# An RWKV and soft-MoE kernel on one core: gathers ahead of the bulk loads, y added by VectorE alone, logits behind the state product, the first slot reordered, the tail in four column groups

## The chip, the core and the metric

The kernel runs on one core of one Trainium2 chip. Its five engines work in parallel, each through its own instruction list in program order: TensorE (PE in the profile; PEld is its weight load), VectorE (DVE), ScalarE (ACT), GpSimd (POOL) and SyncE (SP), which here only issues DMA transfers. An engine waits for another through semaphores. SBUF is the working memory of 128 partitions; PSUM, with 8 banks, takes what TensorE writes. The metric is the time of one execution in microseconds on the device.

## The reference

The inputs are r, k, v, w of shape (4, 8, 768, 48) (batch, head, time, head dimension), u (8, 48), phi (384, 32), w1 (8, 384, 1024) and w2 (8, 1024, 384), all float32.

```
state = 0                                            # per batch and head, 48 x 48
for t in range(768):
    y[t]  = r[t] @ (state + outer(u * k[t], v[t]))
    state = w[t][:, None] * state + outer(k[t], v[t])
x = y as (3072 rows = batch x time, 384 columns = head x dimension)

logits = x @ phi                                     # 3072 x 32 slots, 4 slots for each of 8 experts
d = softmax of logits over the 3072 rows;  slot_input = d.T @ x           # 32 x 384
slot_out[e] = relu(slot_input[e] @ w1[e]) @ w2[e]    # per expert, 4 slots each
c = softmax of logits over the 32 slots;   out = c @ slot_out             # 3072 x 384
```

Both softmaxes add 1e-9 to the sum. The output is stored transposed, 384 x 3072.

## The kernel before, in words

**Attention in 16 slots.** Slot j (0 to 15) works on batch b = j // 4 and on two heads, g = j % 4. Time is cut into 6 chunks of 128 steps. Within a chunk the recurrence is a matrix product: with the running products of w inside a chunk, k is scaled by one (G, from a backward scan, g_scan) and r by another (a forward scan, f_scan), so that the scores of a chunk are k_scaled.T @ r_scaled, masked, and times v; the part across chunks goes through the state at the chunks' ends. w, k and r come in twelve units, three for each batch: a unit has 112 partitions of two heads (48 each, at partitions 0 and 64) and, in the 2 x 16 left-over partitions, a third of two further heads. So slots with g < 3 read a unit's tile directly (kr_b), and slots with g = 3 (3, 7, 11 and 15) read the tile g4, which **gather(n)** (line 516) puts together from the left-over rows of the three units of the batch with two DMAs of 16 rows each, SBUF to SBUF, 96.4 KB a DMA, 24 in all. A gather of unit n has to wait until k and r of unit n are scaled.

**A slot on each engine.** TensorE: the transposes of scaled k (e_kn, line 579, 5 of them), the scores in two halves (e_scores, 589), the sum of k and v per chunk (e_u, 625), the product of the previous slot's masked scores with v (e_av, 648, into the two banks y0 and y1), in some slots the transposes of finished x (x_turn, line 96), the logits (101), the slot product (s_mm, 140), the u-term (e_a, 605), then the previous slot's state product (e_inter, 659, into the same y banks), and one dummy matmul (fill, 497). VectorE: masked copies of three of the four score tiles (598), the state scan (633), reciprocal and forward scan (f_scan, 537 and 538), backward scan (g_scan, 530). ScalarE: evictions from PSUM. The fourth score tile goes by ScalarE (594) and a select on GpSimd (595). GpSimd: r * k (p_rk, 545), k scaled (p_k, 549), r scaled (p_r, 553), v times the u-term (p_av, 620, into the tile av). y of a slot (c_y, 666) is y0 and y1 plus av: ScalarE copies y0 to SBUF (668) and GpSimd adds av to it (670); VectorE adds av to y1 (669).

**Transfers.** All loads but one are issued by SyncE, in program order, into one hardware queue. Per unit: w (387.5 KB, ld_w), k and r (768 KB, ld_kr; the first three units go to other tiles by ld_raw); per slot v (288 KB, ld_v); per expert w1 in three pieces of 512 KB (ld_w1, line 687) and w2 likewise (ld_w2, 690). The tuple PIECES says how many w1 pieces are issued in a slot, in the function weights. A DMA into a tile waits on SyncE's list until the last readers of that tile are done, and all later DMAs of the list wait behind it: w of a unit for c_chk (560, ScalarE, after f_scan) and p_r, v for e_av and p_av, k and r for the state product and the gathers that read the old contents. Unit 0's k and r are issued by ScalarE instead, in two halves, beside SyncE's first loads.

**The MoE part.** The softmax over rows is kept running over the batches (s_max, s_exp, s_sum, s_acc); a batch's logits are computed in the slots of the next batch. After slot 15 comes a chain for the last batch: y (c_y_last), transposes, logits, maximum, exponent, the product d.T @ x, the merge into SI (s_acc), the slot input for the experts (m_slots), the up product (line 224: 8 experts x 3 row blocks x 2 halves of 512 columns), relu and transposes of h (turn, 239), the down product (257) in three groups of 128 columns (COLS), each scaled by the softmax sum (so_scale, 264), spread over partitions (so_rep, 267), and multiplied by the transposed c (mix, 282), copied to SBUF by VectorE and ScalarE (288, 286) and stored. w1 and w2 use SBUF tiles (bin 0 to 15) that the attention part has given free; W1_BINS and W2_BINS say which.

## Time and profile before

| | us |
|---|---|
| median of 3 runs (lowest, highest) | 212.97 (210.42, 213.46) |
| the profiled execution | 212.05 |
| its span in the profile | 210.2 |
| TensorE busy (share of the span) | 177.1 (84%) |
| VectorE busy | 115.7 (55%) |
| GpSimd busy | 104.5 (50%) |
| ScalarE busy | 72.2 (34%) |
| moved by DMA | 51.79 MB, 246 GB/s over the span |

The profile's first page gives busy time by engine, the span in 40 slices with TensorE's granted clock (full speed is 2.4 GHz, the other level 1.2 GHz) and the DMA engines' busy share, the chain of work that ended last, and groups of instructions by source line. Further views are cut from the same execution: tables of busy time in chosen stretches, timelines of one engine with the idle time before a row and what ended it (in brackets), and the times of DMAs from issue to landing. Matmuls overlap, so the time from one row's start to the next row's start says more than a row's own length.

### The profile page before, as it was taken

What the parts mean: (1) busy time and instruction counts of PE and PEld (TensorE: products, weight loads), DVE (VectorE), ACT (ScalarE), POOL (GpSimd) and SP (SyncE); (2) the same over time, 40 slices, a digit from 0 to 9 for tenths busy, and PEclk for the clock granted to TensorE, in tenths of its full rate; (3) what the DMA queues carried; (4) which work ended last, traced back from release to release, by engine and by line L of the source; (5) the groups of instructions that cost most, each with busy time, mean ns of one, the idle gap of its engine ahead of it and who ended that gap; (6) DMA issues with size and microseconds to landing.
All of it is one profiled execution on the core that took longest, in us unless ns stands there. A gap on an engine that the chain in (4) does not pass through costs nothing.

```text
span 210.2 us, 7632 instructions
## 1 busy us (share of the span) xinstructions
PE 177.1 (84%) x3306; PEld 133.2 (63%) x3308; DVE 115.7 (55%) x207; ACT 72.2 (34%) x202; POOL 104.5 (50%) x108
## 2 busy tenths in 40 slices
...
GB/s 177 381 231 298 205 222 303 30 271 168 296 278 305 215 28 362 149 297 263 311 333 85 210 128 323 306 313 385 154 342 416 409 407 260 74 50 254 211 312 93
DMA packets 15176, 51.79 MB, mean 246 GB/s; under 512 B 2208, under 2 KB 2976, under 8 KB 14752
## 3 DMA queue, kind: packets, MB, share of 16 engines
...
q10 hardware_dynamic: 544, 0.79, 1.3%
...
## 4 chain that ended last, share of the span: by engine, by line
PE 54%; DMA 24%; DVE 8%; POOL 5%; issue 2%; SPq 1%; ACT 1%; ACTq 0%; DVEq 0%; POOLq 0%
DMA bin<-bin 14%; PE sc L589 10%; PE y L648 8%; DMA bin<-in_w1l_dram 6%; PE so L257 5%; PE hp L224 5%; DMA bin<-in_krl_dram 4%; PE xp L96 4%; PE up L625 3%; PE kp L579 3%; PE y L659 3%; PE sp L140 3%; PE op L282 2%; POOL bin L553 2%; PE ap L605 2%
## 5 line engine op out<-in xcount | busy, mean ns | idle before, releaser
L589 PE MATMUL sc<-bin 48*128 48x128 f32 x384 | 34.3, 315 | 5.0 <-ACT bin L581 2.8
L589 PEld LDWEIGHTS sc<-bin 48*128 48x128 f32 x384 | 29.4, 215 | 9.7 <-ACT bin L581 4.9
L598 DVE COPY_PREDICATED bin<-later,sc 128x384 f32<-128x384 int32 x49 | 25.3, 581 | 13.4 <-PE sc L589 13.4
L648 PE MATMUL y<-bin,bin 128*64 128x48 f32 x768 | 29.3, 238 | 0.6 <-issue 0.2
L549 POOL TENSOR_TENSOR bin<-bin,bin 128x768 f32<-128x768 f32 (+1 forms) x13 | 20.3, 1563 | 18.7 <-issue 11.6
L648 PEld LDWEIGHTS y<-bin,bin 128*64 128x64 f32 x768 | 27.7, 155 | 1.2 <-ACT bin L668 0.5
L530 DVE TENSOR_TENSOR_SCAN bin<-bin,cst 128x775 f32<-128x775 f32 (+2 forms) x13 | 21.2, 1628 | 2.4 <-DMA bin<-in_wl_dram 2.4
L545 POOL TENSOR_TENSOR bin<-bin 128x768 f32<-128x768 f32 x12 | 21.8, 1819 | 0.1
L538 DVE TENSOR_TENSOR_SCAN bin<-bin,cst 128x774 f32<-128x774 f32 (+1 forms) x13 | 21.4, 1643 | 0.5
L497 PE MATMUL zero<-zb 128*128 128x512 bf16 x58 | 19.8, 443 | 1.5 <-DVE cst L713 1.3
L579 PE MATMUL kp<-ident,bin 112*128 112x112 f32 x80 | 12.0, 287 | 9.3 <-DMA bin<-bin 4.7
L579 PEld LDWEIGHTS kp<-ident,bin 112*128 112x128 f32 x80 | 9.8, 155 | 11.8 <-issue 9.5
L670 POOL TENSOR_TENSOR bin<-bin,bin 128x288 f32<-128x288 f32 x15 | 10.6, 705 | 12.7 <-ACT bin L668 8.0
L620 POOL TENSOR_TENSOR bin<-bin,asb 128x576 f32<-128x576 f32 x12 | 14.0, 1165 | 3.8 <-ACT asb L608 1.7
L581 ACT COPY bin<-kp 128x336 f32<-128x336 f32 (+1 forms) x32 | 11.1, 397 | 13.4 <-PE kp L579 13.4
L595 POOL TENSOR_SCALAR_AFFINE_SELECT bin<-bin 128x384 f32<-128x384 f32 x15 | 7.8, 520 | 15.8 <-ACT bin L594 15.8
L594 ACT COPY bin<-sc 128x384 f32<-128x384 f32 x15 | 7.2, 478 | 22.4 <-PE sc L589 21.3
L633 DVE TENSOR_TENSOR_SCAN bin<-up,bin 112x288 f32<-112x288 f32 x16 | 12.0, 748 | 4.5 <-PE up L625 3.9
L553 POOL TENSOR_TENSOR bin<-bin,bin 128x768 f32<-128x768 f32 (+1 forms) x9 | 13.7, 1518 | 0.0
L257 PE MATMUL so<-bin,bin 128*32 128x128 f32 x384 | 12.2, 274 | 0.0
L497 PEld LDWEIGHTS <-zb 128*128 128x128 bf16 x60 | 6.0, 110 | 9.2 <-issue 5.0
L257 PEld LDWEIGHTS so<-bin,bin 128*32 128x32 f32 x384 | 10.2, 110 | 2.0 <-issue 1.7
...
## 6 DMA issues: line engine op xcount, KB each, us to landing
...
bin<-in_wl_dram SPq DMA_DIRECT2D x11, 387.5 KB, 3.3
...
bin<-bin SPq DMA_DIRECT2D x24, 96.4 KB, 7.5
...
```

The source lines that it names most:

```text
L257: nc.tensor.matmul(out=so[32 * g:32 * g + NS, :], lhsT=hT[ft // 2].rearrange("p (f e s) -> p f e s", f=2, e=E)[:, ft % 2, e, :], rhs=w2t[e ...
L497: nc.tensor.matmul(out=z, lhsT=zb[:, 0:P], rhs=zb, start=True, stop=True)
L530: nc.vector.tensor_tensor_scan(out=G[:, a:z][:, ::-1], data0=wt[:, a:z][:, ::-1], data1=cst[:, 0:1].broadcast_to([P, z - a]), initial=1.0, ...
L538: nc.vector.tensor_tensor_scan(out=wt[:, a:z], data0=wt[:, a:z], data1=cst[:, 1:2].broadcast_to([P, z - a]), initial=1.0, op0=ALU.mult, op ...
L545: nc.gpsimd.tensor_tensor(out=rk_b[n % 2], in0=raw(n)[:, 0:S], in1=raw(n)[:, S:2 * S], op=ALU.mult)
L549: nc.gpsimd.tensor_tensor(out=io[0], in0=io[1], in1=chunks(G_b[n % 2], 2, lo, hi), op=ALU.mult)
L553: nc.gpsimd.tensor_tensor(out=io[0], in0=io[1], in1=chunks(w_b[n % 2], 0, lo, hi), op=ALU.mult)
L579: nc.tensor.transpose(out=kp[:, c - lo, :], in_=kr[0:PITCH, P * c:P * c + P], identity=ident[0:PITCH, 0:PITCH])
L589: nc.tensor.matmul(out=sc[h][:, c, :], lhsT=kr[head(h), lo:lo + P], rhs=kr[head(h), S + lo:S + lo + P], start=True, stop=True)
L598: nc.vector.copy_predicated(out=at, mask=later.broadcast_to([P, HC, P]), data=sc[h])
L620: nc.gpsimd.tensor_tensor(out=av, in0=vt(j), in1=a, op=ALU.mult)
L648: nc.tensor.matmul(out=yb[h][rows, c, :], lhsT=at[:, rows], rhs=vt(j)[:, h, c, :], start=(c == 0), stop=False)
```

## The change

Seven edits, none of which changes what is computed up to rounding order.

1. *Transfers.* In the slot loop, k and r (now of the unit used by slot j - 2) and the weight pieces are issued at the head of a slot, right after e_kn, and w and v later in the slot as before. In slots with g = 1 the weight pieces come at the slot's end instead, and the gather of the third unit, which was in the next slot, comes just ahead of them. PIECES is spread anew (21 pieces as before).
2. *y by VectorE.* c_y is two VectorE additions from PSUM; ScalarE's copy and GpSimd's addition are gone.
3. *Logits behind the state product.* In slots with g = 1 the logits, the maximum, the exponent and e_a come after e_inter and c_y, in the order logits, e_a.
4. *Within a slot.* f_scan comes after the first two masked copies instead of before them, p_r right behind it; c_ends moves from a slot's end to behind the scores of the next slot; the copy of the state (c_state) is split off from state and comes later on ScalarE. c_state, c_pat and c_chk keep their work.
5. *First slot.* Unit 0's k and r come from a second copy in HBM (kr0, the same numbers with each half of the chunks contiguous) on SyncE's queue, between the two halves of w; 14 filling matmuls instead of 26, and the first slot's transposes, sums and scores are taken apart with filling matmuls between.
6. *Softmax over slots.* The sum takes the 1e-9 from an extra column of the tile ce, in place of one VectorE instruction (173) per batch.
7. *Tail.* The last exponent in two halves; the slot input as two products accumulated in PSUM (old SI times the rescaled factor, and the new product, copied to SBUF, times the factor) in place of the merge and one product; the softmax sum after the first quarter of the up product; the first half's turn inside the last quarter of the up product, the other one inside the down product; the down product ordered by row block over all 8 experts, in halves; four column groups (128, 128, 64, 64), of which the narrow two use mix_narrow, with two output DMAs each, one of them issued by ScalarE.

```diff
-N_FILL0 = 26
-N_START = (4, 4, 4)
+N_FILL0 = 14
+N_START = (4, 4, 6)
-N_CHAIN = 2
-PIECES = (0, 0, 1, 1, 2, 1, 1, 2, 2, 2, 2, 2, 2, 2, 1, 0)
+PIECES = (0, 0, 1, 2, 2, 1, 2, 1, 2, 1, 2, 1, 2, 2, 2, 0)
-COLS = ((0, 128), (128, 256), (256, 384))
+COLS = ((0, 128), (128, 256), (256, 320), (320, 384))
...
@@ -248,17 +271,17 @@
-    def down_proj(hT, so, w2t, cg, a=0, z=2 * FT):
+    def down_proj(hT, so, w2t, cg, half):
         lo, hi = COLS[cg]
-        for n in range(a, z):
-            st_, ft = divmod(n, FT)
-            for g in range(4):
-                e = 4 * st_ + g
-                nc.tensor.matmul(
-                    out=so[32 * g:32 * g + NS, :], lhsT=hT[ft // 2].rearrange(
-                        "p (f e s) -> p f e s", f=2, e=E)[:, ft % 2, e, :],
-                    rhs=w2t[e][:, FT * lo + ft * (hi - lo):FT * lo + (ft + 1) * (hi - lo)],
-                    start=(n == 0), stop=(n == 2 * FT - 1))
+        for ft in range(4 * half, 4 * half + 4):
+            for st_ in range(2):
+                for g in range(4):
+                    e = 4 * st_ + g
+                    nc.tensor.matmul(
+                        out=so[32 * g:32 * g + NS, :], lhsT=hT[ft // 2].rearrange(
+                            "p (f e s) -> p f e s", f=2, e=E)[:, ft % 2, e, :],
+                        rhs=w2t[e][:, FT * lo + ft * (hi - lo):FT * lo + (ft + 1) * (hi - lo)],
+                        start=(ft == 0 and st_ == 0), stop=(ft == FT - 1 and st_ == 1))
...
+    def mix_narrow(cT, rep, o, row, bank):
+        ov = o.rearrange("p (n q t) -> p q n t", q=4, t=P)
+        ops = [bank(q, [P, 3, P], "op") for q in range(4)]
+        for hf in range(2):
+            for q in range(4):
+                nc.tensor.matmul(out=ops[q][HALF * hf:HALF * hf + HALF].rearrange("p n t -> p (n t)"),
+                                 lhsT=rep[32 * q:32 * q + NS, :],
+                                 rhs=cT[32 * q:32 * q + NS, 3 * P * hf:3 * P * hf + 3 * P], start=True, stop=True)
+        for q in range(4):
+            if q % 2:
+                nc.scalar.copy(out=ov[:, q], in_=ops[q])
+            else:
+                nc.vector.tensor_copy(out=ov[:, q], in_=ops[q])
+        nc.sync.dma_start(out=out[row:row + HALF, 0:1536], in_=o[0:HALF])
+        nc.scalar.dma_start(out=out[row:row + HALF, 1536:3072], in_=o[HALF:P])
...
-        nc.scalar.copy(out=dst, in_=ys[j][0])
-        nc.vector.tensor_tensor(out=y_of(j, 1), in0=ys[j][1], in1=av[:, 1], op=ALU.add)
-        nc.gpsimd.tensor_tensor(out=dst, in0=dst, in1=av[:, 0], op=ALU.add)
+        for h in range(2):
+            nc.vector.tensor_tensor(out=y_of(j, h), in0=ys[j][h], in1=av[:, h], op=ALU.add)
...
     ld_w(0, 0, HC)
-    ld_raw(0, 0, HC, nc.scalar)
+    ld_half(0)
     ld_w(0, HC, C)
-    ld_raw(0, HC, C, nc.scalar)
+    ld_half(1)
     ld_w(1)
     ld_raw(1)
...
+    spare = lambda shape, name: own(shape, name, "y1")
+    fill(N_FILL0, spare)
     for hf in range(2):
         g_scan(0, HC * hf, HC * hf + HC)
         f_scan(0, HC * hf, HC * hf + HC)
     g_scan(1)
-    f_scan(1)
     for hf in range(2):
         p_k(0, HC * hf, HC * hf + HC)
         p_r(0, HC * hf, HC * hf + HC)
     c_ends(0)
+    p_k(1)
+    e_scores(0, 0)
+    fill(N_START[0], spare)
+    e_kn(0)
     c_chk(0)
-    p_k(1)
+    f_scan(1)
     p_r(1)
-    c_ends(1)
+    fill(N_START[1], spare)
+    c_pat(0)
+    e_u(0)
+    fill(N_START[2], spare)
+    e_scores(0, 1)
     c_chk(1)
-    for hf in range(2):
-        e_scores(0, hf)
-        fill(N_START[hf])
     ld_w(2)
     ld_w(3)
     ld_kr(3)
...
+        m = unit(j - 2) if j > 1 else None
+        m = m + 4 if m is not None and m + 4 < NU else None
+        nw = {0: n0 + 3, 1: n0 + 4, 3: n0 + 5}.get(g)
+        nw = nw if nw is not None and 4 <= nw < NU else None
         if j > 2:
             p_av(j - 1)
+        if j:
+            e_kn(j)
         if g == 1:
             gather(n0)
             gather(n0 + 1)
-        if g == 2:
-            gather(n0 + 2)
-        if ahead is not None:
+        if m is not None:
+            ld_kr(m)
+        if g != 1:
+            weights(PIECES[j])
+        if j == 1:
             f_scan(ahead)
-        e_kn(j)
         if j:
             e_scores(j, 0)
+            if ahead is not None and j > 1:
+                f_scan(ahead)
+            if ahead is not None:
+                p_r(ahead)
             e_scores(j, 1, ((1, 1), (0, 1))[0:SHARED[j]])
-        c_pat(j)
-        e_u(j)
+        if ends is not None:
+            c_ends(ends)
+        ends = later_g
+        if j:
+            c_pat(j)
+            e_u(j)
         state(j)
         if j:
             e_av(j - 1)
         if ahead is not None:
-            p_r(ahead)
             c_chk(ahead)
-        nw = {0: n0 + 3, 1: n0 + 4, 3: n0 + 5}.get(g)
-        if nw is not None and 4 <= nw < NU:
+        if nw is not None:
             ld_w(nw)
-        if j + 3 < NIT and j > 2:
-            ld_v(j + 3)
-        weights(PIECES[j])
         if g == 0 and pb >= 0:
             x_turn(pb, 1)
         if g == 1 and pb >= 0:
@@ -795,17 +866,16 @@
         if g == 2 and pb >= 0:
             s_dturn(qs[pb], rot)
             s_rows(qs[pb], rot)
-            s_rows_exp(qs[pb])
+            s_rows_exp()
+        c_state(j)
         if 1 <= j <= 2:
             e_a(j - 1)
             p_av(j - 1)
-        if j > 1 and unit(j) is not None:
+        if j + 3 < NIT:
+            ld_v(j + 3)
+        soft = g == 1 and pb >= 0
+        if j > 1 and unit(j) is not None and not soft:
             e_a(unit(j))
-        if g == 1 and pb >= 0:
-            lp = rot([TG, 2, P], "lp")
-            for kt in range(KT):
-                l_mm(kt, xT[:, kt], lp)
-            qs[pb] = s_max(pb, lp)
         if g == 3 and pb >= 0:
             sp = s_mm(x_b[pb % 2], qs[pb], rot)
             s_acc(pb, qs[pb], sp)
@@ -816,26 +886,27 @@
                 p_rk(later_g)
             p_k(later_g)
         if g == 2 and pb >= 0:
-            s_norm(pb, qs[pb])
+            s_norm(pb)
         if j:
             e_inter(j - 1)
             c_y(j - 1)
-        if g == 1 and pb >= 0:
+        if soft:
+            lp = rot([TG, 2, P], "lp")
+            for kt in range(KT):
+                l_mm(kt, xT[:, kt], lp)
+            qs[pb] = s_max(pb, lp)
             s_exp(pb, qs[pb])
             s_keep(qs[pb])
-        if later_g is not None:
-            c_ends(later_g)
+            e_a(unit(j))
         if j == 1:
             p_rk(1)
             p_rk(2)
         if j == 3:
             row_constants()
-        if j < 3:
-            ld_v(j + 3)
         fill(N_FILL[j])
-        m = unit(j - 1) if j else None
-        if m is not None and m + 4 < NU:
-            ld_kr(m + 4)
+        if g == 1:
+            gather(n0 + 2)
+            weights(PIECES[j])
         if j == 13:
             for i in range(KT):
                 ld_w1(E - 1, i)
...
@@ -869,35 +940,41 @@
-    fill(N_CHAIN)
     l_turn(x_b[lb % 2], 2, rot, evict2)
+    fill(2)
     l_mm(2, xT[:, 2], lp)
     q = s_max(lb, lp)
-    s_exp(lb, q)
-    fill(N_CHAIN)
+    s_exp(lb, q, 2)
+    fill(2)
     bc = m_spread(lb, rot)
+    s_dturn_parts(q, rot)
     m_factor(lb, q, bc)
-    s_dturn(q, rot)
-    fill(N_CHAIN)
     s_keep(q)
-    s_sum(lb, q)
+    fill(2)
     sp = s_mm(x_b[lb % 2], q, rot)
+    sT = rot([P, KT, NS], "sT")
+    m_old(q, sT)
...
-    s_acc(lb, q, sp)
-    fill(N_CHAIN)
-    m_slots(q, siT, rot)
-    fill(N_CHAIN)
-    m_den(q, rot)
+    spS = cut(2, X, DM)[0:TG]
+    nc.vector.tensor_copy(out=spS[:, 0:192], in_=sp[:, 0:192])
+    nc.scalar.copy(out=spS[:, 192:DM], in_=sp[:, 192:DM])
+    fill(2)
+    m_new(q, sT, spS)
+    ld_w2(6, 2)
+    m_slots(q, siT, sT)
+    fill(2)
     hps = [own([P, 512], f"hp{n}", f"y{n}") for n in range(2)]
     up_proj(siT, hps[0], w1t, 0, 0)
+    s_sum(lb, q)
+    m_den(q, rot)
...
@@ -931,41 +1007,50 @@
-    o_t = [w1t[2], w1t[3], w1t[4]]
-    sos = [own([P, P], f"so{cg}", ("up", "cst", "up")[cg]) if cg < 2 else None for cg in range(3)]
+    o_t = [w1t[2], w1t[3], w1t[4][:, 0:1536], w1t[4][:, 1536:3072]]
     any_bank = lambda q, shape, name: rot(shape, name)
...
+    sos = {}
+
+    def down(cg, half):
+        if half == 0:
+            sos[cg] = own([P, COLS[cg][1] - COLS[cg][0]], f"so{cg}", ("up", "cst")[cg % 2])
+        down_proj(hT, sos[cg], w2t, cg, half)
+        if half:
+            so_scale(sos[cg], so_sb[:, slice(*COLS[cg])])
 
     def spread(cg):
...
-    down_proj(hT, sos[0], w2t, 0)
-    scale(0)
-    for cg in range(1, 3):
-        if cg == 2:
-            sos[2] = own([P, P], "so2", "up")
-        down_proj(hT, sos[cg], w2t, cg, 0, 5)
-        spread(cg - 1)
-        down_proj(hT, sos[cg], w2t, cg, 5, 10)
-        mix_part(cg - 1, 0, any_bank)
-        if cg == 1:
-            range_check()
-        down_proj(hT, sos[cg], w2t, cg, 10, 15)
-        mix_part(cg - 1, 1, any_bank)
-        down_proj(hT, sos[cg], w2t, cg, 15, 16)
-        scale(cg)
...
+    down(0, 0)
+    c_turn(cT, 3, rot)
+    turn(h_sb, hT, 1, rot)
+    down(1, 0)
+    range_check()
+    down(0, 1)
+    down(1, 1)
+    spread(0)
+    down(2, 0)
+    wide(0, 0)
+    spread(1)
+    down(2, 1)
+    wide(0, 1)
     spread(2)
-    mix_part(2, 0, any_bank)
-    mix_part(2, 1, last_bank)
+    down(3, 0)
+    wide(1, 0)
+    narrow(2)
+    down(3, 1)
+    wide(1, 1)
+    spread(3)
+    narrow(3)
```

Three places of the instruction lists, as the two kernels have them.

SyncE's list around slot 9 (g = 1). bin_100 before and bin_103 after are g4; a row `16x1542 x2` is one gather; the rows in_w1l, in_krl, in_wl and in_vl are weight pieces, k and r, w and v. Before:

```order
L519 DMA bin_100<-bin_98 16x1542 x2
L519 DMA bin_100<-bin_99 16x1542 x2
L503 DMA bin_96<-in_wl_dram 128x775
L514 DMA bin_96<-in_vl_dram 128x576
L687 DMA bin_105<-in_w1l_dram 128x1024 x2
L506 DMA bin_98<-in_krl_dram 128x1536
L519 DMA bin_100<-bin_96 16x1542 x2
```

Now:

```order
L565 DMA bin_103<-bin_101 16x1542 x2
L565 DMA bin_103<-bin_102 16x1542 x2
L547 DMA bin_99<-in_wl_dram 128x775
L560 DMA bin_99<-in_vl_dram 128x576
L565 DMA bin_103<-bin_99 16x1542 x2
L742 DMA bin_108<-in_w1l_dram 128x1024
L550 DMA bin_101<-in_krl_dram 128x1536
```

The batch's last gather has moved from behind the weight pieces and k and r to in front of them.

VectorE's list from the end of slot 7 to the end of slot 8. `x3` and `x2` are masked copies of scores; the scans over bin and cst are g_scan (128x775) and f_scan (128x774), the one of 112x288 is the state; `128x6x48` is an addition of y. Before:

```order
L530 SCALAR_TENSOR_TENSOR bin_100<-bin_97,cst 128x775
L669 TENSOR_TENSOR bin_94<-y_1083,bin_99 128x6x48
L537 RECIPROCAL bin_97<-bin_100 128x6
L538 SCALAR_TENSOR_TENSOR bin_97<-bin_97,cst 128x774
L598 COPY_PREDICATED bin_101<-later,sc 128x384 x3
L633 SCALAR_TENSOR_TENSOR bin_95<-up,bin_95 112x288
```

Now:

```order
L576 SCALAR_TENSOR_TENSOR bin_103<-bin_100,cst 128x775
L725 TENSOR_TENSOR bin_97<-y_1074,bin_102 128x6x48
L725 TENSOR_TENSOR bin_97<-y_1075,bin_102 128x6x48
L653 COPY_PREDICATED bin_104<-later,sc 128x384 x2
L583 RECIPROCAL bin_100<-bin_103 128x6
L584 SCALAR_TENSOR_TENSOR bin_100<-bin_100,cst 128x774
L653 COPY_PREDICATED bin_104<-later,sc 128x384
L688 SCALAR_TENSOR_TENSOR bin_98<-up,bin_98 112x288
```

A second addition of y has come in, and two masked copies stand ahead of the forward scan.

TensorE's list at the end of the up product (hp), where htp are turns of h, ctp turns of c, and so is the down product. Before:

```order
L224 MATMUL hp_2406<-bin_96,bin_94 32x512
L239 MATMUL htp<-ident,bin_102 128x128 x4
L274 MATMUL ctp<-ident,cn 128x128 x3
L239 MATMUL htp<-ident,bin_102 128x128 x4
L257 MATMUL so_2504<-bin_97,bin_102 32x128
```

Now, from the last quarter of the up product on:

```order
L313 MATMUL ctp<-ident,cn 128x128 x3
L262 MATMUL htp<-ident,bin_105 128x128 x4
L247 MATMUL hp_2383<-bin_111,bin_97 32x512
L247 MATMUL hp_2383<-bin_109,bin_97 32x512
L247 MATMUL hp_2383<-bin_110,bin_97 32x512
L247 MATMUL hp_2383<-bin_99,bin_97 32x512
```

The first turns have moved ahead of the last eight matmuls of the up product, which end in the first one of the down product; the turns of the other half come after 32 of those.

## Rows read from the trace of the kernel before

**Rows 1.** Chain of waits, in part: start us, us, what.

```profile
1.48 8.36 DMA bin<-in_krl_dram
...
11.79 1.43 POOL bin L549
...
27.92 6.92 DMA bin<-bin
...
99.27 9.41 DMA bin<-bin
```

**Rows 2.** Stretches: length, busy us (instructions) by engine, clock, DMA share, GB/s.

```profile
16.00:25.20 9.20, 7.71 (x166) 7.15 (x162) 6.43 (x8) 3.31 (x9) 5.02 (x5) 0.81 0.85 253
25.20:32.00 6.80, 6.68 (x195) 6.15 (x187) 4.43 (x6) 2.98 (x8) 6.72 (x7) 1.00 0.80 230
32.00:43.30 11.30, 8.73 (x148) 7.69 (x144) 6.38 (x8) 3.73 (x10) 8.90 (x8) 0.70 0.47 157
...
58.90:65.90 7.00, 7.00 (x171) 6.15 (x167) 4.16 (x8) 4.00 (x12) 4.17 (x4) 1.00 1.05 323
...
79.40:87.10 7.70, 7.13 (x172) 6.31 (x168) 7.61 (x9) 3.65 (x11) 5.75 (x7) 1.00 0.75 283
...
95.40:106.20 10.80, 8.60 (x170) 7.68 (x167) 5.29 (x9) 4.15 (x13) 4.21 (x5) 0.82 0.93 280
```

**Rows 3.** Timeline of TensorE: start us, us, instructions, [idle before <-what ended it].

```profile
34.94 1.16 PE L579 MATMUL kp<-ident,bin 112*128 112x112 f32 x5 [2.57 <-DMA bin<-bin]
...
43.53 0.64 PE L579 MATMUL kp<-ident,bin 112*128 112x112 f32 x5
...
69.99 1.17 PE L579 MATMUL kp<-ident,bin 112*128 112x112 f32 x5 [3.73 <-DMA bin<-in_w1l_dram]
...
79.59 0.64 PE L579 MATMUL kp<-ident,bin 112*128 112x112 f32 x5
...
108.93 1.17 PE L579 MATMUL kp<-ident,bin 112*128 112x112 f32 x5 [2.14 <-DMA bin<-bin]
...
119.45 0.65 PE L579 MATMUL kp<-ident,bin 112*128 112x112 f32 x5
...
143.68 0.67 PE L579 MATMUL kp<-ident,bin 112*128 112x112 f32 x5 [0.81 <-DMA bin<-in_w1l_dram]
...
151.26 0.39 PE L497 MATMUL zero<-zb 128*128 128x512 bf16 x1
```

**Rows 4.** Timeline of SyncE's issues around the end of slot 9.

```profile
94.93 0.33 SPq L503 DMA_DIRECT2D bin<-in_wl_dram  x1
...
96.97 0.90 SPq L687 DMA_DIRECT2D bin<-in_w1l_dram  x2
98.34 0.33 SPq L506 DMA_DIRECT2D bin<-in_krl_dram  x1
98.71 1.14 SPq L519 DMA_DIRECT2D bin<-bin  x2
```

**Rows 5.** Line 519, the gathers: time from issue to landing.

```profile
DMA to landing us min/median/max: 4.6/7.5/9.6
```

**Rows 6.** Timeline of TensorE: scores that waited inside a slot.

```profile
81.68 1.18 PE L589 MATMUL sc<-bin 48*128 48x128 f32 x12 [0.57 <-ACT bin L581]
...
97.98 2.07 PE L589 MATMUL sc<-bin 48*128 48x128 f32 x23 [1.46 <-issue]
```

**Rows 7.** Groups by line: busy us, mean ns | idle before, releasers.

```profile
L669 DVE TENSOR_TENSOR bin<-y,bin 128x288 f32<-128x288 f32 x15 | 6.7, 449 | 7.5 <-PE y L659 3.9 <-POOL bin L620 3.3 <-POOL bin L553 0.3
```

**Rows 8.** Timeline after slot 15, all engines.

```profile
150.53 0.80 PE L659 MATMUL y<-bin,bin 48*64 48x48 f32 x40
...
151.45 25.71 SPq L690 DMA_DIRECT2D bin<-in_w2l_dram  x19
...
176.67 0.66 PE L239 MATMUL htp<-ident,bin 128*128 128x128 f32 x4
...
178.67 5.08 PE L257 MATMUL so<-bin,bin 128*32 128x128 f32 x168
```

155 lines of the change are left out of this document (95 added, 60 removed).

## The prediction

> **What bounds the kernel now.** I read the chain of waits first, then the table of stretches slot by slot, then the timelines of TensorE and of SyncE's queue. The chain [rows 1] is to be read for pieces that are not an engine's work: 8.36 us for the second half of unit 0's k and r at the start, then 6.92 and 9.41 us that end in the transfers of line 519, the gathers. The table of stretches [rows 2] shows what such a transfer costs: slot 3 lasts 11.30 us at a granted clock of 0.70, with the DMA engines busy for 0.47 of it, while slot 2, with all its work in place, lasts 6.80 at full clock. TensorE's timeline [rows 3] places the idle time: before the first transposes of slots 3, 7, 11 and 15 (the slots that work on the gathered tile g4) it sits 2.57, 3.73, 2.14 and 0.81 us, 9.25 in all. After the first three it works at 1.2 GHz for a while, the lower of its two levels. SyncE's timeline [rows 4] shows why: the gather of slot 10 is issued at 98.71, behind two weight pieces (96.97) and 768 KB of k and r (98.34), and TensorE resumes at 108.93. Gathers land 4.6 to 9.6 us after issue, 7.5 in the middle [rows 5]. So the slots are bound by TensorE where nothing is late, and every fourth by a transfer.
>
> The profiled execution took 212.05 us, 1.85 more than its span of 210.2, and lies 0.92 under the median of 212.97. The sum is made against 212.05.
>
> **The gathers.** They stay 24, of 96.4 KB; only their place changes. In slot 10's case the last pair now comes right behind the w load (94.93) and one v load instead of at 98.71, about 2.9 us earlier, and the 2 x 512 + 768 KB that stood ahead come behind it. At the 323 GB/s of slot 6 [rows 2] these 1.84 MB are 5.7 us. It should land at 108.93 - 2.9 - 5.7 = 100.3. Slot 10, which begins near 95.4, could end after slot 6's 7.0 us, at 102.4 [rows 2], so 2.1 us are left over. What it frees, from [rows 3]: slot 7 ran from 69.99 to 79.59, 9.60 us, against 7.58 for slot 15 at full clock (143.68 to 151.26), so 2.02 of slow clock and 3.73 of idleness; slot 11 10.52 - 7.58 = 2.94 and 2.14; slot 3, without the slot product, 8.59 against slot 2's 6.80, 1.8 and 2.57; slot 15 0.81. Sum 16.0. Bounds: 16.0, and half of it if each pair lands at 9.6. **-16.0.** Late next is VectorE (below). The bulk loads that now stand ahead of w in a slot (k and r, then weights) delay w by up to 1.28 to 1.8 MB, 4.0 to 5.6 us at that rate, but are issued at the slot's start, while w waits for c_chk in mid-slot; the cover is those some 6 us of the slot, and without it VectorE's scan would wait.
>
> **Order within a slot.** The copy c_ends waited for a scan and held up the copy of the transposes, which held up the scores: 0.57 us in slot 8 [rows 6], 0.70 in slot 12 alike. It now stands behind both. Slot 1 suffered the same in its 9.20 us at clock 0.81, against 6.80 for slot 2 [rows 2]; 2.4 go. **-3.7**, bounds 0 and -3.7. Slot 10's 1.46 us of idle, ended by nothing the profile shows [rows 6], with the slow clock behind it, makes that slot 10.80 us against slot 6's 7.00 [rows 2]: 3.8 us that the change does not touch. As the same bytes pass in less time I add **+1.0** between the bounds of -3.8 and +3.8, a second such place.
>
> **y by VectorE.** ScalarE's copy and GpSimd's addition go; VectorE gets 15 more additions of 449 ns [rows 7], 6.7 us in all. Its cover is VectorE's idle time: busy 4.43 of 6.80 us in slot 2, 4.16 of 7.00 in slot 6 [rows 2]. In slot 8 there is none, 7.61 of 7.70, so I charge 0.4 in slots 4, 8 and 12: **+1.2**; bounds 0 and +6.7. The waiting addition has the next slot's masked copies queued behind it, and TensorE's next y product waits for its bank.
>
> **Logits behind the state product.** The same matmuls in another order; the logits end where they ended, since what moved ahead and what moved behind are about equally long, and e_a fills the time until ScalarE has freed their bank: **0**, bounds -1.5 and +2, from the 1.46 us that slot 10 lost at this place.
>
> **Start.** The second half of k and r landed at 1.48 + 8.36 = 9.84 us on ScalarE's queue, beside SyncE's [rows 1]. In one queue, behind 0.79 MB, it and what is ahead of it are 1.18 MB, 3.7 us at 323 GB/s, so it is there by about 6.5, when its scan ends. Then unit 1's load is late (2.4 MB, 7.3 us, near 9.6), and p_k of unit 1, which began at 11.79 [rows 1], gains 2.2: **-2.2**, bounds 0 and -3.3. Twelve fewer filling matmuls lie beside these loads and cost nothing, unless the clock falls in the gaps. By the Trainium skill ("DMA: Bandwidth & Descriptors", Issuing engines are not separate DMA queues) DMAs of all issuers run on the same 16 engines, and a second issuer saves only issue time; by that rule the move to one queue gives nothing, and the sum would be 2.2 higher. The trace speaks against reading it so: the order in the queue, not the number of queues, is what changes here, and 8.36 us is far above the 3.7 of its own bytes.
>
> **Tail.** Between the end of the last up product's matmuls and the first down product 2.0 us pass, 176.67 to 178.67 [rows 8], for turns and their waits. One turn now lies inside the up product, the other behind the first half of the down product, whose halves need only half of h. The turns' work stays, so at most 2.0 go. The slot input as two products and the exponent in two parts I take at -0.5, between -1 and +0.5. The third column group becomes two of 64: 256 matmul instructions instead of 128. At 128 columns 168 take 5.08 us, 30 ns each [rows 8]; halved with the columns it would be 15, unchanged 30; the nearest row is the state product's 40 instructions of 48 columns in 0.80 us, 20 ns. I take 20: 256 x 20 - 128 x 30 = +1.3 us, bounds 0 and +3.9. **-1.2** in all, bounds -4 and +3. The Trainium skill ("TensorE: Matmul & The Clock Gate", Part 1) has matmuls start no closer than about 25 ns however narrow they are. By that rule the narrow groups would cost 6.4 us, and the sum would be 1.3 higher. The row disagrees: 20 ns each. The w2 pieces are no bound: 19 are issued from 151.45 on over 25.71 us [rows 8], and the down product, which now wants all eight experts' first pieces at once, comes 25 us behind the same point, with a third of the 19 not wanted until later.
>
> **Sum:** -16.0 - 3.7 + 1.0 + 1.2 + 0 - 2.2 - 1.2 = -20.9; 212.05 - 20.9 = 191.2 us.
>
> **Rivals.**
> - *The gathers still land late.* A pair still waits for p_r, and up to 9.6 us pass to landing [rows 5]. Half of the 16.0 stays: 199.2. Against it: 2.1 us in hand. 0.13.
> - *VectorE becomes the bound.* All 15 additions lie open: + 5.5 more, 196.7; with a little contention 198. For it: slot 8. Against it: slots 2 and 6. 0.09.
> - *Start and narrow groups give less.* If unit 1's load is as late in one queue as in two, the 2.2 are not gained: 193.4. If an instruction of 64 columns costs what one of 128 does, 30 ns, 2.6 more: 193.8; both, 196.0. For it: the first products wait for transfers anyway. Against it: 20 ns in the nearest row. 0.11. The two rules of the Trainium skill named above stand on this side, the second with 192.5.
> - *The change doesn't do what it says, since transfers as a whole are the bound.* The DMA engines were busy for 0.75 to 1.05 of the slots without a gather wait [rows 2]. Then the 16.0 us come back as waits for w, k and r: 207 to 212. Against it: half idle in slot 3, at 157 GB/s. 0.05.
> - *Slower.* Both y banks are now freed by VectorE alone, in program order behind its scans, with av from GpSimd; the next product into them waits. If TensorE sits there as long as in slot 10 (1.46 us), its clock falls as it did there: 3.8 us each. From 7 of 15 slots on it is 191.2 + 26.6 = 217.8, slower than before. Against it: ScalarE's copy too waited, and 0.57 us of idleness cost no clock (1.00 in slot 8). 0.04.
>
> My forecast has 0.55, from 186 to 196 by the bounds of its terms; 0.03 is left for better than 186. The range 184 to 203 takes in all but the two last rivals and the far ends, about 0.15. A measurement of this kernel tells 2% from no change, 208.7 and 217.2 around the median. Faster by over 2%: 0.55 + 0.03 + 0.13 + 0.09 + 0.11, 0.91, and a little less for what I do not see: 0.90. Within: 0.06. Slower: 0.04.
>
> **What would show it.** Right: TensorE's idle time before slots 3, 7 and 11 under 0.5 us with the granted clock at 1.00 there; gathers issued within 2 us of the w load ahead; no wait of scores on the transposes' copy; first transposes of slot 1 near 14 us instead of 16; VectorE's y rows 30 at about 450 ns. Wrong: a first transpose that again waits for a gather; VectorE busy nearly all of slots 8 and 12 with y products waiting for it; scans waiting for w; the narrow groups at 30 ns an instruction.

## The result and the profile after

The changed kernel takes 190.89 us in the median of 4 runs (188.74 to 194.65) against 213.22 for the kernel before in the same comparison (210.42 to 215.63); the ratio is 0.8953, 95% interval [0.884, 0.9067]. 191.2 had been forecast, range 184 to 203. Ratios here leave disturbed executions out; where none is given for an experiment, too few undisturbed ones were left, and its runs are told singly. The profiled execution took 188.74, its span is 186.9, so it is set against the 212.05 and 210.2 of before.

Slot by slot, from the start of one slot's first transposes to the next slot's, in us (slot 15 to its last dummy matmul):

| | to slot 1 | 1 | 2 | 3 | 4 | 5 | 6 | 7 | 8 | 9 | 10 | 11 | 12 | 13 | 14 | 15 | after |
|---|---|---|---|---|---|---|---|---|---|---|---|---|---|---|---|---|---|
| before | 16.22 | 9.25 | 9.47 | 8.59 | 7.31 | 8.28 | 10.87 | 9.60 | 7.74 | 8.25 | 13.35 | 10.52 | 7.87 | 8.40 | 7.96 | 7.58 | 58.94 |
| changed | 14.64 | 7.68 | 7.18 | 6.03 | 9.44 | 11.08 | 6.37 | 8.60 | 6.69 | 8.12 | 6.72 | 8.19 | 6.69 | 8.24 | 6.73 | 7.09 | 57.41 |

The differences sum to -23.3, as the spans do. The table of stretches of the changed kernel (length; busy us and instructions of PE, PEld, DVE, ACT, POOL; granted clock; DMA share; GB/s), for slots 3, 4, 5, 8 and 11, beside [rows 2]:

```profile
29.50:35.53 6.03, 6.03 (x146) 5.41 (x144) 5.24 (x9) 2.98 (x9) 5.84 (x4) 1.00 0.94 337
35.53:44.97 9.44, 7.11 (x169) 6.30 (x168) 8.49 (x14) 3.69 (x11) 9.20 (x10) 0.99 0.98 346
44.97:56.05 11.08, 11.08 (x187) 9.43 (x186) 5.90 (x11) 3.74 (x11) 5.39 (x5) 0.70 0.55 154
71.02:77.71 6.69, 6.69 (x169) 6.06 (x168) 6.66 (x10) 3.07 (x9) 6.45 (x7) 1.00 0.87 295
92.55:100.74 8.19, 7.72 (x158) 5.84 (x156) 8.09 (x15) 3.40 (x11) 4.57 (x4) 1.00 0.81 323
```

Slot 3, 8.59 us after a gather before, takes 6.03 at full clock, TensorE busy throughout. In slot 8 TensorE, VectorE and GpSimd are all busy for 6.45 us or more of 6.69. Slots 4 and 5 are longer than before, and TensorE's timeline shows where, beside [rows 3] and [rows 6] (start us, us, instructions, idle before and what ended it):

```profile
35.53 0.64 PE L634 MATMUL kp<-ident,bin 112*128 112x112 f32 x5
...
42.00 0.68 PE L716 MATMUL y<-Sc,bin 48*64 48x48 f32 x30
44.33 0.37 PE L716 MATMUL y<-Sc,bin 48*64 48x48 f32 x10 [1.66 <-issue]
...
44.97 1.14 PE L634 MATMUL kp<-ident,bin 112*128 112x112 f32 x5
...
64.98 0.94 PE L644 MATMUL sc<-bin 48*128 48x128 f32 x13 [1.06 <-issue]
...
71.02 0.65 PE L634 MATMUL kp<-ident,bin 112*128 112x112 f32 x5
...
100.74 0.65 PE L634 MATMUL kp<-ident,bin 112*128 112x112 f32 x5
```

No first transposes wait any more: the rows at 35.53, 71.02 and 100.74 have no idle time. In slot 4, though, TensorE stops for 1.66 us in the middle of 40 equal products, ended by nothing the profile shows, and works at 1.2 GHz behind it (the transposes at 44.97 take 1.14 us instead of 0.64): a place like slot 10's of before, which itself is gone.

SyncE's timeline around the end of slot 9, beside [rows 4], and the landing times of the gathers (line 565 now), beside [rows 5]:

```profile
84.81 0.33 SPq L547 DMA_DIRECT2D bin<-in_wl_dram  x1
85.25 0.38 SPq L560 DMA_DIRECT2D bin<-in_vl_dram  x1
85.68 1.15 SPq L565 DMA_DIRECT2D bin<-bin  x2
86.86 0.58 SPq L742 DMA_DIRECT2D bin<-in_w1l_dram  x1
87.54 0.40 SPq L550 DMA_DIRECT2D bin<-in_krl_dram  x1
```

```profile
DMA to landing us min/median/max: 2.6/4.2/7.8
```

The gather is issued 0.87 us behind the w load, with the bulk behind it, and gathers land after 4.2 us in the middle instead of 7.5. The group of y additions, beside [rows 7], has 30 rows of 445 ns, against the 449 that were reckoned with. From the timeline of the tail, beside [rows 8] (lines 262 and 280 are turns of h and the down product):

```profile
L725 DVE TENSOR_TENSOR bin<-y,bin 128x288 f32<-128x288 f32 x30 | 12.1, 445 | 5.9 <-PE y L716 3.6 <-POOL bin L675 2.1
```

```profile
153.60 1.92 PE L247 MATMUL hp<-bin,bin 128*32 128x512 f32 x16
155.35 1.93 PE L280 MATMUL so<-bin,bin 128*32 128x128 f32 x64
157.21 0.55 PE L313 MATMUL ctp<-ident,cn 128*128 128x128 f32 x3
...
172.87 1.10 PE L280 MATMUL so<-bin,bin 128*32 128x64 f32 x64
173.90 0.84 PE L321 MATMUL op<-bin 32*128 32x256 f32 x8
```

The down product starts as the last up product ends, where 2.0 us lay between. 64 products of 128 columns take 1.86 us from one row's start to the next one's, 29 ns each; 64 of 64 columns 1.03 us, 16 ns each.

### The profile page after: what moved, and what is told of

Same layout as the page of the kernel before. It is cut to its first block, busy times and chain, and to the rows that moved or that the text cites. A ratio compares the mean times of both kernels' runs of the same rounds, so it can differ in the third digit from the quotient of the medians.

```text
span 186.9 us, 7917 instructions
## 1 busy us (share of the span) xinstructions
PE 165.6 (89%) x3452; PEld 124.9 (67%) x3454; DVE 118.5 (63%) x225; ACT 67.1 (36%) x189; POOL 94.4 (51%) x93
## 4 chain that ended last, share of the span: by engine, by line
## 5 line engine op out<-in xcount | busy, mean ns | idle before, releaser
L644 PE MATMUL sc<-bin 48*128 48x128 f32 x384 | 28.7, 292 | 2.6 <-issue 1.1
L644 PEld LDWEIGHTS sc<-bin 48*128 48x128 f32 x384 | 25.0, 196 | 6.8 <-issue 3.2
L705 PE MATMUL y<-bin,bin 128*64 128x48 f32 x768 | 26.7, 226 | 0.8 <-DVE bin L725 0.7
L705 PEld LDWEIGHTS y<-bin,bin 128*64 128x64 f32 x768 | 25.0, 142 | 1.5 <-DVE bin L725 1.5
L725 DVE TENSOR_TENSOR bin<-y,bin 128x288 f32<-128x288 f32 x30 | 12.1, 445 | 5.9 <-PE y L716 3.6
L734 ACT COPY bin<-xp 128x384 f32<-128x384 f32 x22 | 9.4, 478 | 7.6 <-PE xp L98 7.4
L280 PE MATMUL so<-bin,bin 128*32 128x128 f32 (+1 forms) x512 | 11.8, 247 | 0.0
L660 PEld LDWEIGHTS ap<-ums,bin 128*64 128x64 f32 x288 | 9.4, 137 | 2.8 <-DVE bin L725 1.2
L247 PE MATMUL hp<-bin,bin 128*32 128x512 f32 x96 | 10.9, 595 | 0.0
L660 PE MATMUL ap<-ums,bin 128*64 128x4 f32 x288 | 10.4, 200 | 0.5 <-POOL bin L596 0.5
```

The source lines that it names most:

```text
L280: nc.tensor.matmul(out=so[32 * g:32 * g + NS, :], lhsT=hT[ft // 2].rearrange("p (f e s) -> p f e s", f=2, e=E)[:, ft % 2, e, :], rhs=w2t[e ...
L644: nc.tensor.matmul(out=sc[h][:, c, :], lhsT=kr[head(h), lo:lo + P], rhs=kr[head(h), S + lo:S + lo + P], start=True, stop=True)
L660: nc.tensor.matmul(out=ap[HALF * t:HALF * t + HALF, c, :], lhsT=rk[:, P * c + HALF * t:P * c + HALF * t + HALF], rhs=ums[:, n % 3, :], sta ...
L705: nc.tensor.matmul(out=yb[h][rows, c, :], lhsT=at[:, rows], rhs=vt(j)[:, h, c, :], start=(c == 0), stop=False)
L725: nc.vector.tensor_tensor(out=y_of(j, h), in0=ys[j][h], in1=av[:, h], op=ALU.add)
```

## The experiments

Kernels of one comparison shared their chip and the runs of the kernel before. The changed kernel's own median was 190.89 and, run again beside the kernels with another order of SyncE and with later weights, 191.26 (ratio 0.8946, [0.8661, 0.923]). It was not run again beside the others. What an edit costs there is given against these two medians and against the kernel with two queues at the start, which ran beside some of them and took 190.75.

**SyncE's order, undone.** The edit takes back the place of the gather together with the places of k and r and of the weights.

```diff
-PIECES = (0, 0, 1, 2, 2, 1, 2, 1, 2, 1, 2, 1, 2, 2, 2, 0)
+PIECES = (0, 0, 1, 1, 2, 1, 1, 2, 2, 2, 2, 2, 2, 2, 1, 0)
...
-        m = unit(j - 2) if j > 1 else None
+        m = unit(j - 1) if j else None
...
-        if m is not None:
-            ld_kr(m)
-        if g != 1:
-            weights(PIECES[j])
+        if g == 2:
+            gather(n0 + 2)
...
+        weights(PIECES[j])
...
-        if g == 1:
-            gather(n0 + 2)
-            weights(PIECES[j])
+        if m is not None:
+            ld_kr(m)
```

> The changed kernel with SyncE's order of before alone: the third gather of a batch at the head of the next slot, k and r at a slot's end, weight pieces in mid-slot in the old numbers. All other edits stay. Theory (the gathers' place is worth what the idle time and the slow clock before and after them cost): 190.9 + 16 = 206, with TensorE idle for 2 to 4 us before slots 3, 7 and 11, and a granted clock of 0.5 behind it. Rival 1 (GpSimd freed of one addition a slot scales r earlier, and that is what brings the gathers in): at most 4 us of it come back, 191 to 195. Rival 2 (transfers as a whole are the bound): within 2%, 187 to 195, waits only change their names.

207.67 us (205.98 to 211.33), ratio 0.9753 [0.9593, 0.9912]. TensorE's timeline has the idle time back before slots 3, 7 and 11, with transposes at half clock:

```profile
32.70 1.17 PE L634 MATMUL kp<-ident,bin 112*128 112x112 f32 x5 [3.65 <-DMA bin<-bin]
...
71.61 1.17 PE L634 MATMUL kp<-ident,bin 112*128 112x112 f32 x5 [3.09 <-DMA bin<-in_w1l_dram]
...
108.41 1.17 PE L634 MATMUL kp<-ident,bin 112*128 112x112 f32 x5 [2.27 <-DMA bin<-in_vl_dram]
```

The order is worth 16.4 us against the repeated changed kernel, and both rivals fall. What the gather's place is worth without those of k and r and of the weights was not tried.

**SyncE's order alone**, in the kernel before.

```diff
-PIECES = (0, 0, 1, 1, 2, 1, 1, 2, 2, 2, 2, 2, 2, 2, 1, 0)
+PIECES = (0, 0, 1, 2, 2, 1, 2, 1, 2, 1, 2, 1, 2, 2, 2, 0)
...
+        m = unit(j - 2) if j > 1 else None
...
-        if g == 2:
-            gather(n0 + 2)
+        if m is not None and m + 4 < NU:
+            ld_kr(m + 4)
+        if g != 1:
+            weights(PIECES[j])
...
-        weights(PIECES[j])
...
-        m = unit(j - 1) if j else None
-        if m is not None and m + 4 < NU:
-            ld_kr(m + 4)
+        if g == 1:
+            gather(n0 + 2)
+            weights(PIECES[j])
```

> The kernel before with SyncE's new order alone (gathers ahead of the bulk loads, the new spread of weight pieces). Nothing else of the change. Theory: 213.2 - 16 = 197, idle time before slots 3, 7 and 11 under 0.5 us. Rival 1 (it needs the earlier scaled r of the other edits): the gathers wait on SyncE's list for GpSimd and hold up the loads behind them; 205 to 213. Rival 2 (waits for w, k and r take the place): 209 to 215.

197.94 us (195.62 to 199.85), ratio 0.9321 [0.9015, 0.9628]. No first transposes of slots 3 to 15 wait for a gather; the scores of slots 8 and 12 still wait for ScalarE's copy:

```profile
74.35 1.18 PE L589 MATMUL sc<-bin 48*128 48x128 f32 x12 [0.57 <-ACT bin L581]
...
107.06 1.18 PE L589 MATMUL sc<-bin 48*128 48x128 f32 x12 [0.70 <-ACT bin L581]
```

So this order does not need the other edits, and two thirds or so of the gain are its.

**y by three engines as before.**

```diff
-        for h in range(2):
-            nc.vector.tensor_tensor(out=y_of(j, h), in0=ys[j][h], in1=av[:, h], op=ALU.add)
+        dst = y_of(j, 0)
+        nc.scalar.copy(out=dst, in_=ys[j][0])
+        nc.vector.tensor_tensor(out=y_of(j, 1), in0=ys[j][1], in1=av[:, 1], op=ALU.add)
+        nc.gpsimd.tensor_tensor(out=dst, in0=dst, in1=av[:, 0], op=ALU.add)
```

> The changed kernel with y of a slot made as before: ScalarE copies y0, GpSimd adds av, VectorE adds y1. Theory (the term of the sum was +1.2 for VectorE): 191.1 - 1.2 = 190, VectorE's rows of y 15 instead of 30, busy 6.7 us less. Rival 1 (what counts is GpSimd, whose scaled r the gathers wait for): GpSimd's addition behind each slot delays p_r and with it the gathers, 193 to 195, and idle time comes back before slots 3, 7 and 11. Rival 2 (VectorE's idle time covers the second addition and GpSimd's covers the other): 191 in both.

196.86 us (194.66 to 200.97), ratio 0.9259 [0.9184, 0.9334]: 5.6 to 6.1 us slower than with VectorE alone, where 1.2 faster had been charged. TensorE's transposes of finished x (line 98) wait for line 727, GpSimd's addition, in slots 9, 12 and 13. Slot 9 in the timeline of GpSimd and TensorE, and the rows of the other two:

```profile
83.57 1.82 POOL L596 TENSOR_TENSOR bin<-bin 128x768 f32<-128x768 f32 x1
85.48 1.68 POOL L600 TENSOR_TENSOR bin<-bin,bin 128x768 f32<-128x768 f32 x1
87.11 0.69 POOL L727 TENSOR_TENSOR bin<-bin,bin 128x288 f32<-128x288 f32 x1
87.86 0.87 PE L98 MATMUL xp<-ident,bin 128*128 128x128 f32 x6 [1.08 <-POOL bin L727]
...
111.40 0.87 PE L98 MATMUL xp<-ident,bin 128*128 128x128 f32 x6 [0.48 <-POOL bin L727]
...
119.43 0.87 PE L98 MATMUL xp<-ident,bin 128*128 128x128 f32 x6 [1.08 <-POOL bin L727]
```

The addition stands on GpSimd behind r * k and the scaling of k (3.5 us), and GpSimd has no gap in which to catch up. The gathers came in time, so rival 1 had the size but not the way. The three slots are 1.20, 0.55 and 1.22 us longer than in the changed kernel. Slots 10 and 14 are 0.3 longer each, where the scores wait 0.61 us for ScalarE's copy of the u-term instead of 0.31. Together these are 3.6 us. The rest is not shown to come from y: in the profile it lies in slots 1, 3, 4 and 7, at half clock or in stops of TensorE that nothing in the profile ends, and such stops differ from one execution to the next. In the kernel before, the wait for this addition came to 0.2 us in all, and in that kernel with SyncE's new order alone to 0.4. So it takes more than early gathers to expose it.

**The order within a slot, undone.**

```diff
+        if ahead is not None:
+            f_scan(ahead)
         if j:
             e_kn(j)
...
-        if j == 1:
-            f_scan(ahead)
...
-            if ahead is not None and j > 1:
-                f_scan(ahead)
-            if ahead is not None:
-                p_r(ahead)
...
-        if ends is not None:
-            c_ends(ends)
-        ends = later_g
+        if j == 0:
+            c_ends(1)
...
+        c_state(j)
         if j:
             e_av(j - 1)
         if ahead is not None:
+            p_r(ahead)
             c_chk(ahead)
...
-        c_state(j)
...
+        if later_g is not None:
+            c_ends(later_g)
```

> The changed kernel with the old order inside a slot: the forward scan at the head, r scaled behind the y product, the copy c_ends at a slot's end, the copy of the state right behind the state scan. Theory (the term was -3.7): 191.1 + 3 = 194 (slot 1 keeps its new start, so between 1.3 for slots 8 and 12 alone and 3.7), scores of slots 4, 8 and 12 wait 0.5 to 0.7 us for ScalarE's copy of the transposes. Rival 1: r scaled later delays the gathers as well, 196 to 200, with idle time before slots 3, 7, 11. Rival 2: the order does nothing, since VectorE has to do the same scans in the same slots, 191.

197.77 us (196.28 to 200.28), ratio 0.9351 [0.9286, 0.9415]: 6.5 to 7.0 us, more than the 3.7 charged. TensorE's timeline in slots 1 to 3, and in slot 8:

```profile
17.87 1.18 PE L644 MATMUL sc<-bin 48*128 48x128 f32 x12 [1.93 <-ACT bin L636]
25.11 1.14 PE L634 MATMUL kp<-ident,bin 112*128 112x112 f32 x5
...
35.12 0.65 PE L634 MATMUL kp<-ident,bin 112*128 112x112 f32 x5
...
75.18 1.18 PE L644 MATMUL sc<-bin 48*128 48x128 f32 x12 [0.48 <-ACT bin L636]
```

The scores wait for the copy in slot 8 and, for 0.70 us, in slot 12, as expected, but not in slot 4. In slot 1 they wait 1.93 us where 0.78 is left in the changed kernel, and slot 2 behind it takes 10.01 us, from half-speed transposes on, against 7.18. The unexplained stops stand elsewhere in this profile, too: slots 10 and 11 are 4.1 us longer than in the changed kernel's, slots 4 and 5 4.1 shorter. Rival 1 falls: no slot 3, 7 or 11 waits for a gather.

**Two queues at the start.**

```diff
-        nc.sync.dma_start(out=raw_b[0][:, S * hf:S * hf + S], in_=kr0[hf])
+        nc.scalar.dma_start(out=raw_b[0][:, S * hf:S * hf + S], in_=kr0[hf])
```

> The changed kernel with the two halves of unit 0's k and r issued by ScalarE, beside SyncE's first loads, as before; the rest of the first slot stays new. Theory (the term was -2.2, for the order in one queue): 191.1 + 2.2 = 193.3; the second half lands near 9.8 us instead of near 6.5, and the first transposes of slot 1 come 2 us later. Rival (the rule that all issuers share the same DMA engines, so that a second queue changes nothing): 191, the halves land when they did.

190.75 us (189.62 to 193.94), ratio 0.9023 [0.8964, 0.9082], not told apart from the changed kernel. The profile speaks plainly: the halves land 4.1 and 5.3 us after an issue at 0.8 to 1.3 us, the second one at 6.5 against 7.0 in the changed kernel, and slot 1's transposes start at 14.32 against 14.64. The rival was right. Unit 1's k and r, in the changed kernel, land at 10.69, where they landed at 10.57 in the kernel before, and GpSimd waits for them:

```profile
10.83 1.69 POOL L600 TENSOR_TENSOR bin<-bin,bin 128x768 f32<-128x768 f32 x1 [1.66 <-DMA bin<-in_krl_dram]
```

**The old order of the first slot, with the new loads.**

```diff
-    spare = lambda shape, name: own(shape, name, "y1")
-    fill(N_FILL0, spare)
+    fill(26)
...
+    f_scan(1)
...
+    c_chk(0)
     p_k(1)
-    e_scores(0, 0)
-    fill(N_START[0], spare)
-    e_kn(0)
-    c_chk(0)
-    f_scan(1)
     p_r(1)
-    fill(N_START[1], spare)
-    c_pat(0)
-    e_u(0)
-    fill(N_START[2], spare)
-    e_scores(0, 1)
+    c_ends(1)
     c_chk(1)
+    for hf in range(2):
+        e_scores(0, hf)
+        fill(4)
...
-        if j:
-            e_kn(j)
+        e_kn(j)
...
-        if j:
-            c_pat(j)
-            e_u(j)
+        c_pat(j)
+        e_u(j)
```

> The changed kernel with the first slot's instructions in the old order (26 filling matmuls, the scans and scalings of units 0 and 1 first, then both halves of the scores, then transposes and sums), its loads new: unit 0's k and r in contiguous halves on SyncE's queue. Theory (after the run with two queues: the order, not the loads, makes the start shorter): 191.1 + 1.6 = 192.7, first transposes of slot 1 near 16 us. Rival (the loads make it, the contiguous halves): 191, first transposes of slot 1 near 14.3 us.

190.69 us (188.91 to 192.78), ratio 0.9019 [0.8912, 0.9127]. Slot 1's transposes start at 16.43 instead of 14.64, as theory had it, but slot 2's at 23.25 against 22.32: half of it is gone one slot later, and the whole time does not show it.

**Rows of 1.5 KB for unit 0's k and r.**

```diff
-        nc.sync.dma_start(out=raw_b[0][:, S * hf:S * hf + S], in_=kr0[hf])
+        lo, hi = HC * P * hf, HC * P * hf + HC * P
+        nc.sync.dma_start(out=raw_b[0].rearrange("p (a t) -> p a t", a=2)[:, :, lo:hi], in_=krl[0][:, :, lo:hi])
...
```

The scalings read the tile in the same layout.

> The changed kernel with the two halves of unit 0's k and r read from the same array as all other units, in 2 x 128 rows of 1.5 KB a half instead of 128 rows of 3 KB, still on SyncE's queue and with the new order of the first slot. Theory (the contiguous halves are what let the second one land by 7 us instead of 9.8): the second half lands some 2 us later, first transposes of slot 1 near 16 us, 191.1 + 1.5 to 2 = 193. Rival (neither queue nor layout counts, the new order alone does): 191, transposes at 14.3.

191.78 us (191.05 to 197.27), ratio 0.9072 [0.8996, 0.9148], not told apart from the changed kernel. The second half lands at 8.1 us instead of 7.0, and slot 1's transposes start at 14.90, 0.3 us later and not 2: the layout counts for little.

**Fewer bulk bytes early: the stops.**

```diff
-PIECES = (0, 0, 1, 2, 2, 1, 2, 1, 2, 1, 2, 1, 2, 2, 2, 0)
+PIECES = (0, 0, 0, 0, 0, 2, 2, 2, 2, 2, 2, 2, 2, 3, 2, 0)
```

> The changed kernel with the weight pieces of slots 2, 3 and 4 moved to slots 5 to 13 (two or three a slot), the same 21 in all. It is about the places where TensorE stops in the middle of a group of matmuls with no semaphore to wait for: 1.88 us at 42.45 us and 1.33 us at 63.66 us in the profile of the changed kernel, 1.73 at 96.26 and 0.96 at 104.45 before. Theory: these are late instruction blocks. 16 KB packets of the queue named q8 instruction land once per 256 TensorE instructions, each stop sits at instruction 192 plus a multiple of 256, and ends 1.3 to 1.6 us after such a packet landed; the packet starts 3.5 to 5 us after the boundary before it when the bulk transfers run at 320 GB/s or more, 0.2 to 1.2 us when they rest. With fewer bulk bytes in slots 2 to 4 the stop at 42 us goes, and the slow clock of some 3.4 us behind it: 190.9 - 5 = 186, if no other boundary then falls into a full queue in slots 5 to 13; at the same time another stop may come up there, each 1 to 2 us. Rival 1 (the stop is due to the product itself, a PSUM bank or the evictions): it stays at the same matmul, 190 to 192. Rival 2 (weights moved behind make w1 late for the up product): 193 to 198.

> The changed kernel once more, beside the three others on the same chip: 188.7 to 194.7 by its four runs so far. If the stops of TensorE are late instruction blocks, another execution has them at the same instruction numbers (192 plus a multiple of 256), but not at all of the same boundaries; if they belong to the work at that place, at the same matmuls.

The runs with later weights took 197.57, 187.08, 192.9 and 194.0 us. In the profile the stop in slot 4 is still there, at the same matmul, and longer:

```profile
49.59 0.56 PE L716 MATMUL y<-Sc,bin 48*64 48x48 f32 x10 [3.38 <-issue]
```

As a whole this is neither the theory's 186 nor a proof of rival 1, for the same matmul has the same instruction number in both. The DMA packets speak, though. With no weights in slots 2 to 4, w, v and k and r (1.44 MB) were issued at 40.18 to 41.5; the DMA engines moved 229 GB/s from 44 to 46 us and 51 from 46 to 48, when 6 KB packets of k and r were left in three chains, each packet right behind another. One chain ended at 47.22; a 16 KB packet of the instruction queue started at 47.22, landed at 48.18, and TensorE went on at 49.59. In all fourteen profiles TensorE goes on at the same distance behind such a packet at each of the 49 stops of 0.17 us or more between 20 and 150 us that nothing in the profile ends; five of them:

```
kernel            16 KB packet     TensorE goes on   after landing   stop
before            95.25 -  96.56    97.98             1.42            1.46
changed           41.96 -  42.97    44.33             1.36            1.66
changed           62.57 -  63.46    64.98             1.52            1.06
changed, again    43.46 -  44.44    45.77             1.33            3.03
later weights     47.22 -  48.18    49.59             1.41            3.38
(all 49: 1.28 to 1.70 us after a landing)
```

**TensorE's list made 29 matmuls longer ahead of all this.**

```diff
-N_FILL0 = 14
+N_FILL0 = 11
...
+    z16 = spare([P, 512], "zero")
+    for _ in range(32):
+        nc.tensor.matmul(out=z16[:, 0:16], lhsT=zb[:, 0:P], rhs=zb[:, 0:16], start=True, stop=True)
     fill(N_FILL0, spare)
```

> The changed kernel with 32 dummy matmuls of 16 columns ahead of the first filling matmuls and three of these taken out: TensorE's list is 29 matmuls (58 instructions) longer from there on, and nothing else differs. Theory (TensorE stops where a block of 256 instructions begins that has not come in): the stops move 29 matmuls ahead in the work, from the 31st state product of slot 4 (30 before it, 10 behind) to its second (1 and 39), from the 12th score of slot 7 into the state product or the dummy of slot 6; that in slot 11, behind 17 state products, into the u-term or ahead. The boundary before slot 4's stop moves from behind that slot's scores to its first transposes, ahead of k and r and the weights in the queue, so that its block may come in sooner: 186 to 191. Rival (the stops belong to the work, a bank or a buffer): the same matmuls as before, 30 and 10, 11 and 13, and 191.

192.51 us (189.19 to 194.69), ratio 0.902 [0.8925, 0.9114]. Slot 4's 40 products run through. The stops stand elsewhere:

```profile
36.61 0.26 PE L634 MATMUL kp<-ident,bin 112*128 112x112 f32 x1
38.98 0.54 PE L634 MATMUL kp<-ident,bin 112*128 112x112 f32 x4 [2.11 <-issue]
...
63.48 0.40 PE L716 MATMUL y<-Sc,bin 48*64 48x48 f32 x10 [2.20 <-issue]
```

The changed kernel stopped in slot 4 behind 5 transposes and 24 scores, 29 matmuls in (0.67 us, 1.52 after a 16 KB packet landed, though the profile names a VectorE row for it); now it is behind the first matmul, 28 earlier. The stop at the 12th score of slot 7 stands at slot 6's 31st product, 27 matmuls earlier. (Some matmul records are missing from a trace, so a count is good to one or two.) Counted in matmul and weight-load records from the list's start, that stop stands at 2,210 in the changed kernel, at 2,212 in its repetition and at 2,216 here. The boundary that stopped slot 4's products, now at the second of them, passes without a stop. The work did not change, the numbers did: the stops belong to the numbers. Together with the packets this makes them late instruction blocks. The time did not fall: stops that nothing in the profile ends add up to 6.74 us here, against 2.72 in the changed kernel's profile.

**Weights spread with the k and r loads in view, and both together.**

```diff
-PIECES = (0, 0, 1, 2, 2, 1, 2, 1, 2, 1, 2, 1, 2, 2, 2, 0)
+PIECES = (0, 0, 0, 1, 1, 2, 1, 1, 1, 3, 1, 2, 3, 3, 2, 0)
```

With the 29 matmuls the tuple is this, beside the edit shown above:

```diff
+PIECES = (0, 0, 0, 0, 1, 2, 0, 1, 1, 3, 1, 2, 3, 4, 3, 0)
```

> The changed kernel with the 21 weight pieces spread as 0 0 0 1 1 2 1 1 1 3 1 2 3 3 2 0 over the slots: one piece instead of two wherever k and r of a unit are issued at the same head, more in slots 9, 12 and 13, which load little. Theory (instruction blocks queue behind the bulk bytes issued before them): stops in slots 3, 4 and 7 shorten by the 1.3 to 1.6 us that 512 KB take, since the packet then starts that much earlier, and the slow clock behind slot 4's goes: 186 to 189. Rival 1 (the k and r load of 768 KB with v and w is enough to make the block late, as with no weights at all in slots 2 to 4): stops and time as they were, 190 to 193. Rival 2 (weights that come later delay the up product): over 193.

189.12 us (187.08 to 190.89), ratio 0.8926 [0.8833, 0.9018]. Slot 4's stop has 1.50 us and no slow clock behind it (slot 5 8.11 us against 11.08), slot 7's is 1.08, 1.06 before. The stops do not add up to less than in the changed kernel (3.41 us against 2.72); what is gone is the slow clock. The median is the lowest of all, by 1.6 us or more, but the intervals overlap: it is not shown to be faster than the changed kernel.

```profile
45.08 0.37 PE L716 MATMUL y<-Sc,bin 48*64 48x48 f32 x10 [1.50 <-issue]
...
45.62 0.65 PE L634 MATMUL kp<-ident,bin 112*128 112x112 f32 x5
```

> The changed kernel with both: the 29 matmuls more at the front, and the weight pieces spread as 0 0 0 0 1 2 0 1 1 3 1 2 3 4 3 0. Theory (instruction blocks are asked for at a boundary and queue behind the bulk bytes issued before it): in slots 3, 4, 6 and 7 the boundary now lies within 0.5 us of the first transposes, ahead of k and r, and no weights stand before them in slots 2 and 3; the stops add up to under 1.5 us, no slow clock follows one, 185 to 188. Rival 1 (the v, w and k and r loads alone keep the queue full): stops of 2 to 4 us in all, 188 to 191, as with the spread alone (189.1). Rival 2 (too many weights left to the end: the up or down product waits): tail longer than 64.5 us from the transposes of slot 15, over 190.

192.16, 191.03, 191.5, 187.53, 190.4 and 191.36 us: all but one outside 185 to 188. Slot 4 has no stop, and slot 6 has 2.60 us with half clock behind it; stops add up to 5.94 us in the profile against 3.41 with the spread alone. Where they fall is a matter of which boundary meets which load, and this choice only moved them. That fewer bulk bytes early make the stops shorter as a whole is not shown by any of the three spreads: with later weights they add up to 5.86 us, while the changed kernel has 2.72 and, in its repetition, 4.26.

## Why the prediction was right

The forecast was a gain of 20.9 us against the profiled time; the profile has 23.3. By its own steps:

- *The gathers, -16.0.* Idle time of 9.25 us went to nothing, and slots 3, 7 and 11 lost 2.56, 1.00 and 2.33 besides: 15.1. Undoing SyncE's order cost 16.4. The mechanism and the size hold. That one pair is issued early enough was argued from its own bytes and those ahead; the rows of SyncE show it.
- *Order within a slot, -3.7.* Slots 1, 8 and 12 lost 1.57, 1.05 and 1.18 us: 3.8. The sum holds, its parts less: 2.4 of it had been seen in slot 1, where scores still wait 0.78 us for ScalarE's copy. Undone it cost 6.5 to 7.0, since in the shorter slots the wait in slot 1 is 1.93 us and takes the clock of slot 2 with it.
- *+1.0 for another stop like slot 10's.* Slot 10 lost 4.49 us beside its gather's, slots 4 and 5 gained 4.93: +0.4. The size is luck: slot 10's stop, which the change was not to touch, went, and another came in its place. The cause was unknown when the term was set, and is a late instruction block.
- *y by VectorE, +1.2, and logits, 0.* This step failed. What is left of the slots is -1.7 us (slots 2, 6, 9, 13, 14 and 15 beside the gathers). The prediction costed the addition VectorE gained and put the one GpSimd lost at nothing, without a reason. GpSimd is busy for half the span, but nearly throughout slots 8 and 12 (6.45 of 6.69 us in slot 8, without that addition), and with the addition put back x's transposes in slots 9, 12 and 13 wait for its end. Undoing the edit in the new kernel costs 5.6 to 6.1 us, of which 3.6 are shown as waits for GpSimd and ScalarE. VectorE's side was as told: waits of TensorE for y's banks are 0.42 and 0.31 us, far from the 1.46 of the slower rival. The logits were not tried alone; slots 9 and 13, which hold them, lost 0.13 and 0.16 us.
- *Start, -2.2.* 1.58 in the profile, but the reason given is wrong. Not the one queue: the halves land no later with two. Not, but for 0.3 us, the layout. Unit 1's load, told to be in near 9.6 us, landed at 10.69, and at 10.57 in the kernel before: the condition of the rival on the start came true, and p_k of unit 1 begins at 10.83 instead of 11.79, 1.0 us earlier and not 2.2. The first slot's order makes slot 1 start 1.8 us earlier, of which 0.9 is left in slot 2 and nothing measurable at the end. The Trainium skill ("DMA: Bandwidth & Descriptors", Issuing engines are not separate DMA queues) had it right, and the 8.36 us of [rows 1] were read as the price of the order in the queues without being tried. Why that half landed so late in the kernel before stays open: ScalarE's queue and the rows of 1.5 KB were put back one at a time, not together.
- *Tail, -1.2.* 1.53. Up to the up product 0.09 us are gained, where the slot input and the exponent had been taken at -0.5; from there to the first down product 1.46; behind it nothing. The 2.0 us between up and down product are gone as told, but one turn now lies inside the up product. The narrow columns cost 256 x 16 - 128 x 29 = +0.4 us instead of +1.3; the rule of about 25 ns at least ("TensorE: Matmul & The Clock Gate", Part 1, of the Trainium skill) does not hold here, where the products go in turn to four groups of 32 output rows.

So the sum came out within 2.4 us of the profile while the start had the wrong reason and y the wrong sign. That the median of 190.89 lies 0.3 us from the forecast is luck. The parts do not add: undone one at a time, SyncE's order, the order within a slot and y cost 28 to 30 us together, more than the whole gain of 22.3 to 24.5, and each of these runs has stops of its own. Some waits come up only when others are gone: the one for GpSimd's addition grew from 0.2 us to three waits of 2.64 in all. The softmax sum and the tail were not tried alone.
